# One kernel of attention, routed experts and a dense MLP: first group's rows gathered and prepared between conversions, two accumulations of the second product run beside the first group

## The chip, the cores and the metric

One Trainium2 chip, one core. The metric is the device time of one execution in microseconds (us), as the median of several runs. The engines: PE (TensorE: matmuls, and PEld its weight loads), DVE (VectorE), ACT (ScalarE), POOL (GpSimd), SP (SyncE, here a queue that issues DMAs).

## What is computed

```python
x = attention(q, k, v)                  # 4 batches, 12 heads, 448 rows, causal
# 8 experts, each row goes to the one with the largest gate logit
out[mask] = gate_w * eom * (relu(x[mask] @ w1[e]) @ w2[e])
# dense MLP on the 1792 rows of 768
h = out @ w_in                          # 768 -> 2048
g = h - tanh(h)
y = g @ w_out                           # 2048 -> 768
```

Weights come as 64-bit floats and are converted on the chip. A product of two matrices is done as three products of 16-bit planes (hi x hi, hi x lo, lo x hi), so every operand has a high and a low plane.

## The kernel before, in words

The kernel runs attention, then the experts one after the other in slots of 128 rows, then the dense MLP. The order of instructions on every engine is written by hand (`manual_schedule`): an engine takes its instructions in the order in which the program text issues them.

Beside the experts w_in and w_out are converted: 24 blocks of 128 x 1024 numbers, the first 12 of w_in, the rest of w_out. `conv` makes one block: three DVE operations put the 64-bit words together in the one buffer `cc` (`to_f32`, L896 to L902), `scaled` makes the high plane (L113 on ACT, L117 on DVE), `rest_of` the low plane (L115 and L129 on POOL, or L121 on DVE). `conv_store` writes both planes to the DRAM tensor `wb_d`; `wi_load` and `wo_load` bring quarters of w_in and w_out back. `remaining()` converts, in a loop whose length comes from the data, what the experts had no time for; here the loop is not entered. The last two blocks of w_out (q = 0, 1) are loaded from POOL's queue (1 MB each) and converted straight into w_out's buffer; q = 0 uses `cc` as well.

The last expert (e = 7) has its optional slots filled by `fill(z)`: fill(1) converts unit 0, fill(2) issues the two POOL loads and converts unit 1, fill(3) is `first_prep`. Rows of the first group of the MLP pass through prep0 (gather of sorted rows, SP, L971), prep1 (three reduces L982 and small operations, DVE), prep_hi (ACT, L996), prep_lo (POOL, two pairs L1010 and L1012 a block of rows), prep_sc, prep2 (transposes on PE, L149, and copies L151, L153) and prep3 (row scales through PE, L1036).

The MLP runs over five groups of 128-row blocks, GB = (3, 3, 3, 3, 2). Its loop has 16 steps n a group, one for each 128 of the 2048 columns. `a_mm(n)` (L1222) is 18 matmuls of 128 x 384 for h; `act_a` multiplies by the row scale into `cc` (L1230, called h below), squares and tanh go on ACT, V and X on POOL (L1232, L1235); `act_b`, `act_c` evaluate a polynomial on DVE (L1242, L1248, L1250) and write the high plane of g, `act_d` its low plane (L1258; POOL for group 0). The pool of h's PSUM has two buffers, so a_mm(n+2) waits for h of n. `mm2_step` (L1273) is three matmuls of 384 columns for y, one k of one accumulation; a group of three blocks has 2 x 3 x 16 = 96 of them, in six accumulations one after the other. They run one group behind the first product: while group 1's a_mm go, the 96 steps of group 0 are spread over its steps n = 17 to 31 (LAG = 1). So PE has no second product during group 0. While group 0 runs, group 1's rows are prepared (prep1 at n = 0, prep_hi and prep_lo at n = 1 to 7, prep2 at 9 to 11, prep3 at 12 and 13).

## Time and profile before

| | before |
|---|---|
| three runs, us | 1048.73, 1044.98, 1041.18 (median 1044.98) |
| the profiled execution, us | 1040.45 |
| its span, us | 1038.7 |
| PE busy | 984.5 us, 95% |
| DVE busy | 786.6 us, 76% |
| ACT busy | 596.7 us, 57% |
| POOL busy | 472.2 us, 45% |
| mean granted clock of PE | 0.993 |
| DMA, mean | 167 GB/s |

The span is the time between the first and the last instruction of the one execution that was profiled; the runs' times include what lies around it. Busy shares are averages over stages with different limits, so a stage has to be read by itself. Attention and experts fill the first 574 us, the MLP the rest.

### The profile page before, as it was taken

The numbers are of one execution on the slowest core, as the hardware profiler recorded it, in microseconds if no ns is written. First come the engines' busy times: TensorE is split into PE (matmuls) and PEld (weight loads), VectorE is DVE, ScalarE is ACT, GpSimd is POOL, SyncE is SP. The second block draws the span as 40 slices with busy tenths as digits, with TensorE's granted clock in tenths as the row PEclk, the third lists the DMA queues.
The fourth block names the chain that finished last, engine by engine and source line by source line (L and its number), as shares of the span: only waits on it lengthen the run. The fifth ranks groups of instructions, "written<-read, shape, count | busy, mean of one in ns | idle before, by whom it ended". The sixth has DMA issues, their size and how long they took to land. (4 is left out here: it accounts for less than half of the span.)

```text
span 1038.7 us, 24100 instructions
## 1 busy us (share of the span) xinstructions
PE 984.5 (95%) x9177; PEld 743.4 (72%) x9177; DVE 786.6 (76%) x1609; ACT 596.7 (57%) x1194; POOL 472.2 (45%) x499
## 2 busy tenths in 40 slices
PE   5999999998998999999988889999999999999996
PEld 4999999996876878777865555666666666667763
DVE  6668778786786778778877899887888798776640
ACT  5777776764456366564332679555656566555530
POOL 5475876585311011102137789545544443443321
PEclk9999999999999999999999999999999999999999
DMA  8989997963888979977987514010011000000000
GB/s 240 234 216 270 241 266 202 240 197 126 303 342 316 351 268 333 363 291 239 317 299 280 209 62 157 24 47 16 24 31 32 9 31 9 16 16 17 16 24 23
DMA packets 62646, 173.92 MB, mean 167 GB/s; under 512 B 8368, under 2 KB 23344, under 8 KB 59424
## 3 DMA queue, kind: packets, MB, share of 16 engines
q1 hardware_dynamic: 56352, 147.20, 42.7%
q0 software_dynamic: 6144, 24.84, 8.3%
q8 instruction: 79, 1.29, 0.5%
q14 instruction: 71, 0.58, 0.2%
HBM read 132.30 MB, written 29.62 MB: 156 GB/s over the span
## 5 line engine op out<-in xcount | busy, mean ns | idle before, releaser
L1273 PE MATMUL fo<-wo,g 128*128 128x384 f16 x1344 | 228.2, 326 | 0.0
L1222 PEld LDWEIGHTS <-raw 128*128 128x128 f16 x1440 | 140.7, 98 | 87.9 <-issue 9.5
L1273 PEld LDWEIGHTS <-g 128*128 128x128 f16 x1344 | 131.2, 98 | 83.8
L1232 POOL TENSOR_TENSOR V<-cu,cc 128x384 f32<-128x384 f32 (+1 forms) x80 | 78.7, 984 | 189.0 <-ACT cu L1231 188.2
L162 PEld LDWEIGHTS <-w 128*128 128x128 f16 x2592 | 148.9, 99 | 15.5 <-issue 14.4
L1222 PE MATMUL fh<-cu,raw 128*128 128x384 f16 (+1 forms) x864 | 131.9, 308 | 5.7 <-DVE cc L1230 5.7
L344 ACT ACTIVATE P<-s,nb 112x112 f32<-112x112 f32 (+1 forms) x192 | 89.9, 495 | 56.5 <-DVE nb L338 27.9
L381 PE MATMUL o<-v,PT 112*112 112x65 f32 x960 | 114.6, 259 | 0.0
L381 PEld LDWEIGHTS o<-v,PT 112*112 112x112 f32 x960 | 105.4, 178 | 0.1
L121 DVE SCALAR_TENSOR_TENSOR w<-raw,w 128x768 f16<-128x768 f32 (+1 forms) x99 | 99.1, 1061 | 3.6 <-ACT w L113 3.6
L799 POOL DMA_INDIRECT xg<-xs_d,idx x22 | 27.5, 1249 | 162.2 <-PEq L871 21.6
L1231 ACT ACTIVATE cu<-cc 128x384 f32<-128x384 f32 (+1 forms) x80 | 40.1, 502 | 101.9 <-DVE cc L1230 101.9
L1235 POOL TENSOR_TENSOR X<-cc,X 128x384 f32<-128x384 f32 (+1 forms) x80 | 91.2, 1141 | 4.1 <-ACT X L1234 0.5
L1230 DVE TENSOR_TENSOR cc<-fh,co 128x384 f32<-128x384 f32 (+1 forms) x80 | 42.0, 526 | 66.3 <-PE fh L1222 50.7
L113 ACT ACTIVATE w<-raw 128x768 f16<-128x768 f32 (+2 forms) x106 | 89.0, 904 | 5.5 <-DVE xi L758 3.2
L331 DVE TENSOR_REDUCE s<-s 112x2 f32<-112x224 f32 (+1 forms) x144 | 78.9, 548 | 14.8 <-PE s L327 12.7
L1242 DVE SCALAR_TENSOR_TENSOR V<-cu,V 128x384 f32<-128x384 f32 (+1 forms) x80 | 85.3, 1066 | 0.1
L1250 DVE TENSOR_TENSOR V<-V,co 128x384 f32<-128x384 f32 (+1 forms) x64 | 78.4, 1224 | 0.0
L1222 PE MATMUL fh<-yh,raw 128*128 128x384 f16 x384 | 67.6, 326 | 0.7 <-DVE cc L1230 0.7
L1251 ACT ACTIVATE g<-V 128x384 f16<-128x384 f32 (+1 forms) x80 | 40.1, 501 | 46.9 <-DVE V L1250 46.7
L362 PE MATMUL t<-ident,P 112*112 112x112 f32 x480 | 66.7, 262 | 0.0
L325 PE MATMUL s<-kh,qa 128*112 128x112 f16 (+1 forms) x192 | 54.7, 293 | 12.7 <-POOL qa L276 7.4
(657 smaller groups left out, 2038.8 us busy)
## 6 DMA issues: line engine op xcount, KB each, us to landing
raw<-w SPq DMA_DIRECT2D x48, 512.0 KB
raw<-w SPq DMA_DIRECT2D x60, 384.0 KB
cu<-wf SPq DMA_DIRECT2D x22, 1024.0 KB
wb_d<-co SPq DMA_DIRECT2D x22, 512.0 KB
raw<-kq SPq DMA_DIRECT2D x11, 896.0 KB
raw<-wb_d SPq DMA_DIRECT2D x8, 768.0 KB
xs_d<-xq SPq DMA_DIRECT2D x24, 224.0 KB
raw<-v SPq DMA_DIRECT2D x11, 448.0 KB
```

Source lines behind the costliest of these rows:

```text
L113: nc.scalar.activation(out=out, in_=in_, func=AF.Copy, scale=WS)
L121: nc.vector.scalar_tensor_tensor(out=out, in0=in_, scalar=WS, in1=hi, op0=ALU.mult, op1=ALU.subtract)
L162: nc.tensor.matmul(out=ph[:, (f % 4) * 128 : (f % 4 + 1) * 128], lhsT=w[0][:, ww, k, f * 128 : (f + 1) * 128], rhs=xTs[tag][:, xx, k, :], ...
L331: nc.vector.tensor_reduce(out=d["nm", m], in_=d["s", m], op=ALU.max, axis=AX.X, negate=True)
L344: nc.scalar.activation(out=d["P"][:, j, OFF[i] : OFF[i] + n], in_=d["s", m][:, z, :], func=AF.Exp, bias=d["nb"][:, 2 * i + j : 2 * i + j + ...
L381: nc.tensor.matmul(out=po[:, i, :], lhsT=d["PT"][:, g, o : o + CP], rhs=d["t"][3][:, hl, j, :], start=(j == 0), stop=(j == i))
L1222: nc.tensor.matmul(out=ph[:, 0:nt], lhsT=wi[ww][:, f // 4, k, f % 4 * 128 : (f % 4 + 1) * 128], rhs=yy[:, k, 0:nt], start=(q == 0), stop=( ...
L1232: nc.gpsimd.tensor_tensor(out=d["V"], in0=d["U"], in1=d["h"], op=ALU.mult)
L1235: nc.gpsimd.tensor_tensor(out=d["X"], in0=d["h"], in1=d["X"], op=ALU.subtract)
L1242: nc.vector.scalar_tensor_tensor(out=d["V"], in0=d[f"S{z}"], scalar=QD[z - 1], in1=d["V"], op0=ALU.add, op1=ALU.mult)
L1250: nc.vector.tensor_tensor(out=d["V"], in0=d["V"], in1=rs_y(g, nt), op=ALU.mult)
L1273: nc.tensor.matmul(out=po[:, 0:384], lhsT=t[:, x, k, i * 128 : (i + 1) * 128], rhs=wo_[ww][:, k, z * 384 : (z + 1) * 384], start=(k == 0 a ...
```

## The change

1. The three gathers of group 0 (prep0) are issued ahead of `remaining()`, whose scratch moves to another place (`spo`).
2. The fills of the last expert: fill(2) issues the two POOL loads and does `first_prep`; the conversion of unit 1 follows in fill(3).
3. Behind the last expert, the low planes of the last two blocks are made by DVE behind prep2 and prep3 instead of by POOL; `oidx` (the store addresses, two small POOL operations) is made in `order_b`.
4. The PSUM pool of the transposes has one buffer for each of two tags instead of two of one tag; `ro` takes one of them. prep2 of group 1 is done one plane a step at n = 7 to 12.
5. The order of the second product: the first 32 steps are two accumulations side by side (blocks 0 and 1, first half of the columns), two steps at each of n = 5 to 20. Their weights for k < 12 come from a copy of the first 384 columns of w_out in the buffer of g of group 1 (`wc_load`, four DMAs behind n = 0 and n = 1, 2.4 MB). The other 64 steps of group 0 are spread over n = 21 to 31. `wo_load` runs at n = 14 to 17, last quarter first, instead of n = 12 to 15.

```diff
     flg = cst.tile([1, 4], I32, name="flg")
+    oidx = cst.tile([128, NBLK, 2], U32, name="oidx")
...
-    def planes_T(rows, hi, lo, pool, tag="t", eng="a"):
-        for x, dst in enumerate((hi, lo)):
-            pt = pool.tile([128, 1024], F16, tag=tag, name=f"pt_{nc.get_next_instruction_name()}")
+    def planes_T(rows, hi, lo, pool, tag="t", eng="a", xs=(0, 1)):
+        for x in xs:
+            dst = (hi, lo)[x]
+            pt = pool.tile([128, 1024], F16, tag=tag[x % len(tag)], name=f"pt_{nc.get_next_instruction_name()}")
             pv = pt[:, 0:DM].rearrange("p (k n) -> p k n", k=KD)
...
-    def prep2(g, i, tag="t"):
+    def prep2(g, i, tag="t", xs=(0, 1)):
         d = G[g % 2]
         tsl = slice(i * 128, (i + 1) * 128)
-        planes_T(yq_of(g, i), d["yh"][:, :, tsl], d["yl"][:, :, tsl], tpool[0], tag, "v" if g == 1 else "a")
+        planes_T(yq_of(g, i), d["yh"][:, :, tsl], d["yl"][:, :, tsl], tpool[0], tag, "v" if g == 1 else "a",
+                 xs)
...
         nc.vector.tensor_reduce(out=smt[:, :, 1:2], in_=pv[:, :, 2:5], op=ALU.add, axis=AX.X)
+        for z in range(2):
+            nc.gpsimd.tensor_scalar(out=oidx[:, :, z], in0=smt[:, :, 0], scalar1=2.0, scalar2=float(z), op0=ALU.mult,
+                                    op1=ALU.add)
...
                 conv_load(stg[0], o)
-                conv(stg[0], stg[2][:, 0:1024], stg[2][:, 1024:2048])
+                conv(stg[0], spo[:, 0:1024], spo[:, 1024:2048])
                 nc.sync.dma_start(out=wb_d[:, :, ds(o, 1), :].rearrange("p a o n -> p a (o n)"),
-                                  in_=stg[2][:, 0:2048].rearrange("p (a n) -> p a n", a=2))
+                                  in_=spo.rearrange("p (a n) -> p a n", a=2))
...
             stg = [wof[0][:, z * 4096 : (z + 1) * 4096].bitcast(U32).rearrange("p (n t) -> p n t", t=2) for z in range(2)]
-            stg += [wof[1][:, z * 2048 : (z + 1) * 2048] for z in range(2)]
-            tot = nc.values_load(flg[0:1, 1:2], min_val=0, max_val=NDY)
-            remaining()
+            spo = wof[0][:, 8192:10240]
             first["yg"] = [wof[1][:, z * 2 * DM : (z + 1) * 2 * DM].bitcast(F32) for z in range(3)]
...
                 prep0(0, i, second * i if i else 0)
+            tot = nc.values_load(flg[0:1, 1:2], min_val=0, max_val=NDY)
+            remaining()
...
                         conv_load(stg[q], NDY + q, nc.gpsimd)
-                if z in (1, 2):
-                    conv(cu[z - 1], co[z - 1][:, 0], co[z - 1][:, 1], "p")
-                    conv_store(z - 1, nc.values_load(flg[0:1, z + 1 : z + 2], engines=(SP,), min_val=0, max_val=NDY - 1))
-                if z == 3:
                     first_prep()
+                if z in (1, 3):
+                    b = z // 2
+                    conv(cu[b], co[b][:, 0], co[b][:, 1], "p")
+                    conv_store(b, nc.values_load(flg[0:1, b + 2 : b + 3], engines=(SP,), min_val=0, max_val=NDY - 1))
...
         scaled("v", qhl[q][0], qc[q].bitcast(F32))
-        if q:
-            for prep in (prep2, prep3):
-                for i in range(GB[0]):
-                    tpool[0] = (mp_t, mp_y, mp_h)[i]
-                    prep(0, i, "tys"[i])
-        rest_of("p", qhl[q][1], qc[q].bitcast(F32), qhl[q][0])
+    for prep in (prep2, prep3):
+        for i in range(GB[0]):
+            tpool[0] = (mp_t, mp_y, mp_h)[i]
+            prep(0, i, "tys"[i])
+    for q in range(2):
+        rest_of("v", qhl[q][1], qc[q].bitcast(F32), qhl[q][0])
...
     fp_o = wctx.enter_context(tc.tile_pool(reuse_waits="tile", name="fp_o", bufs=2, space=PSUM))
-    tpool[0] = wctx.enter_context(tc.tile_pool(reuse_waits="tile", name="fp_t", bufs=2, space=PSUM))
-    oidx = yp.tile([128, NBLK, 2], U32, name="oidx")
-    for z in range(2):
-        nc.gpsimd.tensor_scalar(out=oidx[:, :, z], in0=smt[:, :, 0], scalar1=2.0, scalar2=float(z), op0=ALU.mult, op1=ALU.add)
+    tpool[0] = wctx.enter_context(tc.tile_pool(reuse_waits="tile", name="fp_t", bufs=1, space=PSUM))
     Q = {}
-    ro = fp_o.tile([128, 512], F32, tag="o", name="ro")
+    ro = tpool[0].tile([128, 512], F32, tag="r", name="ro")
     for i in range(GB[0]):
...
     steps = [(g, i, z, k) for g in range(len(GB)) for z in range(2) for i in range(GB[g]) for k in range(KF2)]
-    cur = [None]
+    KC = 12
+    AHEAD = {n: 2 for n in range(5, 21)}
+    steps[0:32] = [(0, i, 0, k) for k in range(KF2) for i in range(2)]
+    steps[32:96] = [(0, i, z, k) for i, z in ((2, 0), (0, 1), (1, 1), (2, 1)) for k in range(KF2)]
+    acc = {}
+    def wc_load(k0, k1):
+        for x in range(2):
+            src = wb_d[:, x, NI : NI + KC * DM // 1024, :].rearrange("p a n -> p (a n)").rearrange("p (k n) -> p k n", n=DM)
+            nc.sync.dma_start(out=gt[1][:, x, k0:k1, :], in_=src[:, k0:k1, 0:384])
     late = []
...
         if k == 0:
-            cur[0] = fp_o.tile([128, 512], F32, tag="o", name=f"fo_{bk}_{z}")
-        po = cur[0]
+            acc[bk, z] = fp_o.tile([128, 512], F32, tag="o", name=f"fo_{bk}_{z}")
+        po = acc[bk, z]
         t = gt[g % 2]
         for x, ww in ((0, 0), (0, 1), (1, 0)):
-            nc.tensor.matmul(out=po[:, 0:384], lhsT=t[:, x, k, i * 128 : (i + 1) * 128],
-                             rhs=wo_[ww][:, k, z * 384 : (z + 1) * 384], start=(k == 0 and x == 0 and ww == 0),
+            w = gt[1][:, ww, k, :] if bk < 2 and z == 0 and k < KC else wo_[ww][:, k, z * 384 : (z + 1) * 384]
+            nc.tensor.matmul(out=po[:, 0:384], lhsT=t[:, x, k, i * 128 : (i + 1) * 128], rhs=w, start=(k == 0 and x == 0 and ww == 0),
                              stop=(k == KF2 - 1 and x == 1))
...
             a_mm(n)
-            if n in (9, 10, 11):
-                prep2(1, (9, 10, 11).index(n))
+            if 7 <= n < 13:
+                prep2(1, (n - 7) // 2, xs=((n - 7) % 2,))
             for i in {12: (0, 1), 13: (2,)}.get(n, ()):
...
             wi_load(nc.sync, f + 1)
-        if g == 0 and f in (12, 13, 14, 15):
-            wo_load(nc.sync, f - 12)
+        if n in (0, 1):
+            wc_load(n * 4, 4 + n * 8)
+        if 14 <= n < 18:
+            wo_load(nc.sync, (3, 0, 1, 2)[n - 14])
         if 0 < g < len(GB) - 1:
...
                 if f == (5, 8, 12)[i]:
-                    prep2(g + 1, i)
+                    prep2(g + 1, i, "tr")
                 if f == (6, 9, 13)[i]:
                     prep3(g + 1, i)
-        if okf(n) and g >= 1 and f >= LAG:
-            tot = GB[g - 1] * 2 * KF2
-            q0 = tot * (f - LAG) // (KF2 - LAG)
-            q1 = tot * (f - LAG + 1) // (KF2 - LAG)
+        for _ in range(AHEAD.get(n, 0)):
+            mm2_step()
+        lag = 5 if g == 1 else LAG
+        if okf(n) and g >= 1 and f >= lag:
+            tot = GB[g - 1] * 2 * KF2 - (sum(AHEAD.values()) if g == 1 else 0)
+            q0 = tot * (f - lag) // (KF2 - lag)
+            q1 = tot * (f - lag + 1) // (KF2 - lag)
             for _ in range(q1 - q0):
...
```

On POOL, in the last expert's fills, before (co is the buffer of a converted unit, wo_17684 the buffer that holds the gathered rows and their planes):

```order
L906 DMA wo_17683<-wf 128x2048 x2
L115 TENSOR_SCALAR scm<-cc 128x512
L129 TENSOR_TENSOR co_4959<-scm,co_4959 128x512
L115 TENSOR_SCALAR scm<-cc 128x512
L129 TENSOR_TENSOR co_4959<-scm,co_4959 128x512
L1010 TENSOR_SCALAR scm<-wo_17684 128x384
L1012 TENSOR_TENSOR wo_17684<-scm,wo_17684 128x3x128
```

and now, up to the same conversion (lines are numbered two or one higher):

```order
L1012 TENSOR_SCALAR scm<-wo_17687 128x384
L1014 TENSOR_TENSOR wo_17687<-scm,wo_17687 128x3x128
L1012 TENSOR_SCALAR scm<-wo_17687 128x384
L1014 TENSOR_TENSOR wo_17687<-scm,wo_17687 128x3x128
L116 TENSOR_SCALAR scm<-cc 128x512
L130 TENSOR_TENSOR co_4960<-scm,co_4960 128x512
L116 TENSOR_SCALAR scm<-cc 128x512
L130 TENSOR_TENSOR co_4960<-scm,co_4960 128x512
```

The low half of unit 1's conversion stood ahead of all prep_lo pairs; now it is the last of them, and no low half of the last two blocks follows on POOL.

On SP, before, from the end of `remaining()` on (UNCONDITIONAL_BRANCH closes it; wo_17684 as above, ys_d the experts' rows):

```order
L1077 UNCONDITIONAL_BRANCH
L1126 TENSOR_LOAD flg
L1126 ISA x2
L971 DMA wo_17684<-ys_d 128x768
L971 ISA
L971 DMA wo_17684<-ys_d 128x768
L971 ISA
L971 DMA wo_17684<-ys_d 128x768
```

and now, up to the branch that opens it:

```order
L973 DMA wo_17687<-ys_d 128x768
L973 ISA
L973 DMA wo_17687<-ys_d 128x768
L973 ISA
L973 DMA wo_17687<-ys_d 128x768
L1133 TENSOR_LOAD flg
L1133 ISA x2
L1083 COMPARE_AND_BRANCH
```

The three gathers moved from behind the conditional loop to ahead of it.

On PE, in group 0, before, at the end of a_mm(5) (fh_5) and the start of a_mm(6) (each LDWEIGHTS loads the weights of the matmul behind it):

```order
L1222 LDWEIGHTS raw1_89
L1222 MATMUL fh_5_19711<-cu_1_4956,raw1_89 128x384
L1222 LDWEIGHTS raw1_89
L1222 MATMUL fh_5_19711<-cu_1_4956,raw1_89 128x384
L1222 LDWEIGHTS raw1_89
L1222 MATMUL fh_6_19747<-cu_0_4955,raw1_89 128x384
L1222 LDWEIGHTS raw1_89
L1222 MATMUL fh_6_19747<-cu_0_4955,raw1_89 128x384
```

and now, at the end of a_mm(5) (g_0 is g of group 0, g_1 the buffer with the copy of w_out; fo_0 and fo_1 are the two accumulations):

```order
L1225 LDWEIGHTS raw1_90
L1225 MATMUL fh_5_19709<-cu_1_4957,raw1_90 128x384
L1225 LDWEIGHTS raw1_90
L1225 MATMUL fh_5_19709<-cu_1_4957,raw1_90 128x384
L1287 LDWEIGHTS g_0_19483
L1287 MATMUL fo_0_0_19745<-g_1_19484,g_0_19483 128x384
L1287 LDWEIGHTS g_0_19483
L1287 MATMUL fo_0_0_19745<-g_1_19484,g_0_19483 128x384
L1287 LDWEIGHTS g_0_19483
L1287 MATMUL fo_0_0_19745<-g_1_19484,g_0_19483 128x384
L1287 LDWEIGHTS g_0_19483
L1287 MATMUL fo_1_0_19749<-g_1_19484,g_0_19483 128x384
```

Six matmuls of the second product stand between a_mm(5) and a_mm(6), and likewise behind each a_mm up to n = 20.

## Rows read from the trace of the kernel before

**Rows 1.** Windows: us; busy PE, PEld, DVE, ACT, POOL (instructions); granted clock, DMA share, GB/s

```profile
600.00:620.00 20.00, 17.55 (x126) 10.78 (x124) 20.00 (x33) 15.66 (x32) 17.48 (x16) 1.00 0.19 71
...
640.00:660.00 20.00, 20.00 (x125) 12.04 (x123) 18.82 (x36) 13.52 (x27) 13.12 (x12) 1.00 0.07 21
```

**Rows 2.** Waits of PE, 540 to 650 us: total us, times, longest

```profile
PE fh L1222 <- DVE cc L1230: 6.3, 8, 1.6
PE py_I-18271_18272 L174 <- ACT hh_I-18095_18096 L169: 4.1, 1, 4.1
```

**Rows 3.** Timeline of PE in group 0: start us, us, line, operation, [idle before]

```profile
591.35 3.08 PE L1222 MATMUL fh<-cu,raw 128*128 128x384 f16 x18 [1.65 <-DVE cc L1230]
...
609.21 0.50 PE L149 MATMUL pt_I-19869_19870<-identh,wo 128*128 128x128 f16 x6
...
621.93 0.27 PE L1036 MATMUL rsp_I-20025_20026<-wo,onesb 128*128 128x256 bf16 x1
...
632.89 2.11 PE L1222 MATMUL fh<-yh,raw 128*128 128x384 f16 x12 [0.35 <-DVE cc L1230]
```

**Rows 4.** Timeline of DVE, lead-in and start of group 0, columns as above

```profile
541.13 0.75 DVE L896 TENSOR_SCALAR cc<-cu 128x512 uint32<-128x512 uint32 x2
541.80 1.29 DVE L899 SCALAR_TENSOR_TENSOR cc<-cu,cc 128x512 uint32<-128x512 uint32 x2
...
555.48 0.95 DVE L982 TENSOR_REDUCE wo<-wo 128x1 f32<-128x768 f32 x1 [2.96 <-DMA wo<-ys_d]
...
562.83 0.69 DVE L896 TENSOR_SCALAR cc<-wo 128x1024 uint32<-128x1024 uint32 x1 [0.45 <-DVEq L871]
...
572.62 0.69 DVE L117 TENSOR_SCALAR wo<-wo 128x1024 f16<-128x1024 f32 x1
...
574.17 0.55 DVE L151 COPY cu<-pt_I-19457_19458 128x768 f16<-128x768 f16 x1
577.72 0.56 DVE L1230 TENSOR_TENSOR cc<-fh,co 128x384 f32<-128x384 f32 x1 [3.00 <-POOL scm L115]
...
590.75 0.54 DVE L1230 TENSOR_TENSOR cc<-fh,co 128x384 f32<-128x384 f32 x1
```

**Rows 5.** Timeline of POOL, the same stretch

```profile
559.61 0.59 POOL L1010 TENSOR_SCALAR scm<-wo 128x384 f32<-128x384 f32 x1
560.28 0.91 POOL L1012 TENSOR_TENSOR wo<-scm,wo 128x384 f16<-128x384 f32 x1
...
564.06 1.76 POOL L1012 TENSOR_TENSOR wo<-scm,wo 128x384 f16<-128x384 f32 x1
...
573.12 0.68 POOL L115 TENSOR_SCALAR scm<-cc 128x512 f32<-128x512 f32 x1 [1.61 <-DMA xg<-xs_d,idx]
...
579.73 1.16 POOL L129 TENSOR_TENSOR wo<-scm,wo 128x512 f16<-128x512 f32 x1
...
581.21 0.98 POOL L1232 TENSOR_TENSOR V<-cu,cc 128x384 f32<-128x384 f32 x1
...
594.16 1.63 POOL L1258 TENSOR_TENSOR g<-V,g 128x384 f16<-128x384 f32 x1
```

**Rows 6.** Timeline of SP, its DMA issues

```profile
546.61 1.56 SPq L971 DMA_DIRECT2D wo<-ys_d  x3
549.25 11.26 SPq L917 DMA_DIRECT2D wb_d<-co  x2
...
563.43 0.83 SPq L955 DMA_DIRECT2D raw<-wb_d  x2
```

**Rows 7.** Waits of SP's queue, 540 to 600 us

```profile
SPq L1077 <- SPq L1077: 4.0, 1, 4.0
```

**Rows 8.** Windows around PE's idle stretch ahead of the slot, columns as in group 1

```profile
558.00:560.00 2.00, 0.00 (x0) 0.00 (x0) 1.72 (x6) 2.00 (x3) 1.50 (x3) 1.00 0.18 68
...
562.00:563.00 1.00, 1.00 (x5) 0.48 (x4) 0.55 (x2) 0.00 (x0) 0.90 (x2) 0.50 1.05 395
```

**Rows 9.** Line L121 on DVE, 300 to 560 us: duration ns min/median/max

```profile
L121 DVE SCALAR_TENSOR_TENSOR co<-cc,co x32: 684/692/693, 311.5 to 530.7; 128x512 f16<-128x512 f32 x32
```

## The prediction

> **What bounds the kernel now.** I read the busy table by stretches first. From 640 us on PE is busy 20.00 of 20 us, and 125 matmuls of 384 columns fill the stretch: 0.16 us each [rows 1]. Nothing but less PE work, or PE idle time taken out ahead of it, can shorten the rest of the kernel. Between 600 and 620 us PE is busy 17.55 and DVE 20.00: there, in group 0, DVE is the bound [rows 1]. The waits of PE between 540 and 650 us then show what there is to win: 6.3 us in eight waits of fh for h (the DVE operation at L1230), and one wait of 4.1 us for hh, the relu of the last expert's second slot [rows 2]. PE's timeline places the first kind: blocks of 18 matmuls of 3.08 us, with gaps such as 1.65 us ahead of n=5 and still 0.35 us at n=16, which starts at 632.89 [rows 3]. Last I followed the lead-in on DVE, POOL and SP [rows 4 to 6].
>
> Group 0 starts with h0 at 577.72, after 3.00 us in which DVE waited for POOL's scm L115 [rows 4]: h is written to the buffer cc, which POOL still reads for the low half of the last converted w_out block. POOL's eight operations for that run from 573.12 to 580.9, and V of n=0 begins only at 581.21 [rows 5].
>
> **Gathers ahead of the conditional loop.** SP waits 4.0 us at the branch of `remaining()` [rows 7], ahead of the three gathers, the first of which goes out at 546.61 [rows 6]. Behind the change they leave about 4.5 us earlier, near 542. The third reduce now begins at 555.48, after a DMA wait of 2.96 us [rows 4], beside two 1 MB loads from POOL's queue; without these beside them I take the reduces as done by 549 and the scales by 550. (With the old 8.9 us from first issue to third reduce, 551.)
>
> **prep ahead of conversion 1.** ACT's prep_hi then ends near 552.5, DVE's conversion of unit 1 runs behind it, and hh comes near 557. The wait of 4.1 us [rows 2] goes, and with it the half clock: after PE stood empty at 558 to 560 us its granted clock was 0.50 at 562 to 563 us [rows 8]. Slot 7.2 thus ends some 5 us earlier. That is worth nothing by itself: what starts group 0 is the work behind it on DVE.
>
> POOL now runs six prep_lo pairs, then the low half of conversion 1. A pair takes 0.59 + 0.91 us plus gaps, 1.6 [rows 5]; conversion 1 takes 2 x (0.68 + 1.16) = 3.7 by the rows of the same operations [rows 5]. From 550 that is 550 + 9.6 + 3.7 = 563.3, with gaps 564. Beside DVE's long two-input operations the second half of a pair took 1.76 instead of 0.91 [rows 5]; if all six were stretched so, with the first halves in proportion, it is 6 x 2.9 + 3.7 = 21, hence 571. DVE's overlapping work is now mostly one conversion, not two blocks, so I take X = 566 for POOL's end, bounds 564 and 571.
>
> [...]
>
> **Conversions of the last two blocks.** DVE's to_f32 of q=0 overwrites cc, so it now waits for X. Uncontended, two blocks cost 2 x (0.75 + 1.29 + 1.29 + 0.69) = 8.0 us [rows 4]; before they took 562.83 to 573.3, 10.4 us [rows 4]. Then three copies of yl (0.55 each, 0.47 apart: 1.5 us [rows 4]) and the two rest_of moved from POOL: 0.69 us per 512 columns [rows 9], hence 1.3 each, 2.6 together. h0 comes at X + 12.1 = 578.1, against 577.72: **not earlier**, +0.4. Under the bounds of X it is 576.1 to 583.1.
>
> PE stands idle some 6 us ahead of a_mm(0), and the row above says that it then runs some us at half clock; the 12 matmuls that need only yh can start when w_in's first quarter has landed, so this is covered by the DVE work as long as that quarter comes by 574. SP issues it behind the store of conversion 1 (X + 0.3 = 566.3) and that store's landing. Before, the load at 563.43 followed 2.9 us after the issues of the stores ended (549.25 + 11.26 = 560.5) [rows 6]; so 569.5, and 1.57 MB at the 1 MB per 2.6 us of the neighbouring stretch (395 GB/s, [rows 8]) takes 4.0: 573.5 to 575. It is close, and costs at most 1.5 us.
>
> What POOL's freedom buys: V of n=0 follows its square at once instead of at 581.21, and the small DVE operations of group 1's prep1 no longer share with POOL. I put 1.0 us on that, so h of n=3 (590.75 [rows 4]) comes at 590.75 + 0.4 - 1.0 = 590.15.
>
> **The 32 ahead steps.** A step is three matmuls: 0.48 us. 22 of them stand at n=5 to 15, two per n, 10.6 us of work taken out of group 1, where PE is full [rows 1]. In group 0 PE then needs per n 18 + 6 matmuls, 2.9 + 0.97 = 3.87 us; eleven of them 42.6, with six batches of transposes of 0.50 and three rs matmuls of 0.27 (3.8 us, [rows 3]) 46.4. DVE's part per n is as before. So PE becomes the bound of group 0. From h3, a_mm(5) starts 0.6 later; to the 46.4 I add 1.5 for two stalls: the first ahead step needs the low plane of g(0), whose POOL operation stood at 594.16 and took 1.63 [rows 5], about as long as a_mm(5) now lasts; and the transposes have one PSUM buffer per tag instead of two. a_mm(16) starts at h3 + 48.5; before it was 632.89 - 590.75 = 42.1. So n=16 comes 6.4 later relative to h3 with 10.6 us of work done: gain 4.2.
>
> At n=16 to 20 ten more steps are taken. They only fill the gaps there (0.35 twice and the smaller, together 0.9 [rows 3]); I give 0.5 back for DVE being late at n=18 with group 2's preparation. The cost of the extra loads of w_out's half, 2.4 MB on SP's queue between the quarters of w_in: 6 us at the rate above. The second quarter goes first, the third is needed at n=8, the last at n=12, some 20 to 40 us later: hidden. Were it not hidden PE would wait up to 6 us at n=4.
>
> **Sum**: +0.4 (h0) - 1.0 (n=0 to 3) - 4.2 (n=5 to 15) - 0.9 + 0.5 = -5.2, rounded to -5. The profiled execution took 1040.45 us, 1.7 over its span; it lies 4.5 under the median of 1044.98 and 0.7 under the lowest. I forecast the median: 1044.98 - 5 = 1040.
>
> **Rivals.**
> (a) *Start later, nothing gained.* POOL's prep_lo and conversion 1 are stretched, X is 569 to 571, h0 3 to 5 us later. For it: 1.76 for 0.91 [rows 5]. Against: less DVE work beside it. Time 1043 to 1045.
> (b) *Slower.* The same chain, one mechanism: cc is now held by conversion 1 on POOL, DVE's last two blocks and the two rest_of lie serially behind it. It decides from an h0 over 5.2 us later, X beyond 571.2; that needs prep_lo to start after 550 too, as with the old landing. X = 573 gives 1047.
> (c) *The ahead steps gain nothing*: each step pair waits for a late low plane of g, because POOL, stretched by DVE, runs its act_d behind V and X (1.63 rather than 0.91). Group 0's PE idle stays, only elsewhere. Against: five n lie between g's start and its use. Only the start terms are left: 1044 to 1046.
> (d) *Start really earlier*: hh 5 us earlier carries through, with X at 564 or below and DVE's copies and rest_of partly in its own gaps. h0 at 573 to 576, 2 to 5 us ahead of my 578.1: -7 to -10; with neither of the two stalls of 1.5 us in all down to -12: 1033 to 1038.
>
> [...] Were a_mm(0) not covered by DVE's work, it would take 6.2 instead of 3.08 us, h0 would be 2 us later, and the gain 3 instead of 5.
>
> **How the numbers follow.** Forecast (-2 to -8): 0.54. (a) 0.15, (c) 0.09, (b) 0.09, (d) 0.13. One per cent, 10.4 us, is about what a measurement of this kernel can tell from no change: its three runs lie 7.5 us apart. Faster by over 1%: the better half of (d) and some luck in the median, 0.11. Slower by over 1%: only the tail of (b), X past 581, 0.04. Within: 0.85. The range reaches from 1032 (most of (d)) to 1046 (all of (a), part of (b) and (c)); the forecast's own is 1037 to 1043.
>
> **What would show it.** Right: hh without its 4.1 us wait; the first gather near 542; h0 within 2 us of 578; V of n=0 right behind its square; PE over 19 of 20 us between 600 and 640, and DVE under 20. Wrong: h0 past 583 (a, b) or before 576 (d); PE gaps that end on a POOL subtraction of g ahead of the ahead steps (c); a wait of fh for a load at n=0 or 4.

## The result and the profile after

The changed kernel is slower: 1055.26 us in the median of 17 runs against 1045.69 for the kernel before in its own 17, ratio 1.0078 with an interval of 1.0054 to 1.0102 (the ratio is not the quotient of the two medians, which is 1.0092). That is 8 to 10 us more, where 5 less were forecast, and outside the range of 1032 to 1046. All ratios here leave out executions in a slower state, among them two of ahead_short's twelve and one of start_early_nocc's at 1276 to 2627 us; the one trace of ahead_short is of such an execution, of 1056.99 us.

The profiled executions were 1055.61 (span 1053.9) and 1040.45 us (span 1038.7), 15.2 apart. The first lies at its median, the second 5 below its own, so some 5 of the 15.2 are scatter. Both traces have 9177 matmuls in the same stages. At the first matmul of the second product of the last expert's first slot (py of slot 7.1), called a below, the changed kernel is 2.9 us behind, in stages that the change hardly touches. The rest arises behind a.

The windows that answer [rows 1] (us; busy PE, PEld, DVE, ACT, POOL; granted clock, DMA share, GB/s), with the lead-in and group 1's start:

```profile
560.00:580.00 20.00, 12.06 (x80) 6.99 (x81) 14.12 (x17) 6.79 (x12) 14.00 (x15) 0.74 0.31 117
580.00:600.00 20.00, 15.55 (x90) 8.54 (x87) 13.37 (x23) 7.85 (x17) 4.30 (x4) 0.91 0.72 269
600.00:620.00 20.00, 17.26 (x110) 10.23 (x108) 20.00 (x38) 16.88 (x33) 16.35 (x14) 1.00 0.75 271
...
660.00:680.00 20.00, 15.48 (x103) 9.41 (x101) 18.07 (x34) 12.71 (x25) 11.89 (x11) 1.00 0.07 21
```

and of the kernel before:

```profile
560.00:580.00 20.00, 18.17 (x124) 10.79 (x125) 15.72 (x18) 7.57 (x16) 16.98 (x18) 0.91 0.65 231
...
660.00:680.00 20.00, 20.00 (x134) 12.32 (x132) 16.66 (x30) 11.17 (x22) 11.17 (x10) 1.00 0.06 21
```

Two things stand out: a lead-in in which PE is busy for 12.06 and 15.55 of 20 us, at a mean granted clock of 0.74 and 0.91, and a hole at 660 to 680 us, where PE was full before. The waits of PE from 535 us to the end (total us, times, longest) name both; the first and the third row answer [rows 2]:

```profile
PE py_I-18274_18275 L176 <- ACT hh_I-18098_18099 L171: 7.9, 1, 7.9
PE fo L1287 <- ACT ot L1291: 4.9, 1, 4.9
PE fh L1225 <- DVE cc L1233: 3.4, 3, 1.7
PE fh L1225 <- DMA raw<-wb_d: 2.3, 2, 1.4
...
PE fo L1287 <- POOL g L1261: 1.1, 1, 1.1
```

The wait for hh has not gone, it has doubled. The eight waits for h are three. New are two waits for the DMA of w_in's first quarter and one of 4.9 us for ot, the write-out of finished accumulations by ACT.

**The lead-in.** SP's timeline, in two pieces, then on (compare [rows 6]):

```profile
546.82 1.21 SPq L973 DMA_DIRECT2D wo<-ys_d  x2
...
553.10 0.35 SPq L973 DMA_DIRECT2D wo<-ys_d  x1
...
555.54 20.30 SPq L919 DMA_DIRECT2D wb_d<-co  x2
...
579.30 0.82 SPq L957 DMA_DIRECT2D raw<-wb_d  x2
```

The gathers go out ahead of the conditional loop, but the third leaves 5 us after the second. The store of conversion 1 ends its issue at 575.84, and w_in's first quarter is asked for at 579.30. POOL's timeline, against [rows 5]:

```profile
558.81 0.58 POOL L1012 TENSOR_SCALAR scm<-wo 128x384 f32<-128x384 f32 x1 [2.63 <-PE ph_I-18180_18181 L164]
...
573.59 1.67 POOL L130 TENSOR_TENSOR co<-scm,co 128x512 f16<-128x512 f32 x1
590.52 1.00 POOL L1235 TENSOR_TENSOR V<-cu,cc 128x384 f32<-128x384 f32 x1 [15.25 <-ACT cu L1234]
```

POOL starts its six pairs at 558.81, ends conversion 1 at 575.26 and then has nothing to do for 15 us. DVE's timeline, against [rows 4]:

```profile
556.67 0.95 DVE L984 TENSOR_REDUCE wo<-wo 128x1 f32<-128x768 f32 x1 [1.92 <-DMA wo<-ys_d]
...
573.54 0.70 DVE L898 TENSOR_SCALAR cc<-wo 128x1024 uint32<-128x1024 uint32 x1 [4.50 <-POOL scm L116]
...
584.63 1.22 DVE L122 SCALAR_TENSOR_TENSOR wo<-wo 128x1024 f16<-128x1024 f32 x1
589.26 0.56 DVE L1233 TENSOR_TENSOR cc<-fh,co 128x384 f32<-128x384 f32 x1 [3.42 <-PE fh L1225]
592.26 2.67 DVE L984 TENSOR_REDUCE wo<-wo 128x1 f32<-128x768 f32 x3 [2.44 <-SPq L873]
```

DVE waits 4.50 us until POOL has read cc (L116), is through with the last blocks at 585.85, and then waits another 3.42 us for a_mm(0). PE's timeline and its clock say why (compare [rows 3, 8]):

```profile
583.33 1.15 PE L1225 MATMUL fh<-cu,raw 128*128 128x384 f16 x6 [1.43 <-DMA raw<-wb_d]
585.36 9.65 PE L1225 MATMUL fh<-cu,raw 128*128 128x384 f16 x48 [0.88 <-DMA raw<-wb_d]
...
680.69 4.28 PE L1287 MATMUL fo<-wo,g 128*128 128x384 f16 x15 [4.91 <-ACT ot L1291]
```

```profile
586.00:588.00 2.00, 2.00 (x7) 0.88 (x6) 0.00 (x0) 0.00 (x0) 0.00 (x0) 0.50 0.76 297
```

a_mm(0) waits for the two planes of w_in, at 583.33 and 585.36, and then runs at a granted clock of 0.50 (586 to 588 us), after four microseconds, 582 to 586, in which PE was busy for 1.8.

**The hole behind a_mm(21).** DVE and ACT there (n = 19's h is the second DVE row; n = 20's chain on ACT begins at 676.34):

```profile
666.93 0.94 DVE L984 TENSOR_REDUCE co<-co 128x1 f32<-128x768 f32 x1
...
671.43 0.55 DVE L1233 TENSOR_TENSOR cc<-fh,co 128x384 f32<-128x384 f32 x1
```

```profile
676.34 0.52 ACT L1234 ACTIVATE cu<-cc 128x384 f32<-128x384 f32 x1 [0.41 <-DVE cc L1233]
...
680.08 1.03 ACT L1291 ACTIVATE ot<-fo,usc 128x384 f32<-128x384 f32 x2
```

a_mm(19) ends near 666.9, but DVE then does prep1, prep_lo and prep_sc of group 2 and comes to h(19) only at 671.43. ACT follows DVE, and its two ot stand in its order behind the chain of n = 20. Both accumulation buffers are held until ACT comes to them; PE, through with a_mm(21) and two batches of transposes, stands for 4.91 us and goes on at 680.69.

**Stages.** The table is worked out from the timelines of each kernel: a is the start of PE's first matmul of py of slot 7.1, h0, h3, ... are the starts of DVE's h operation (L1230; L1233 in the changed kernel), the end is the start of PE's last matmul (1029.70 before, 1044.86 after). us, one execution each; the ratio is that of the timed runs to those of the kernel before, with its 95% interval.

| kernel | ratio | a to h0 | h0 to h3 | h3 to h16 | h16 to h21 | h21 to h31 | h31 to end |
|---|---|---|---|---|---|---|---|
| before | 1 | 37.8 | 13.0 | 48.4 | 24.3 | 62.8 | 303.5 |
| before_again | | 35.7 | 13.7 | 48.4 | 24.2 | 62.8 | 303.5 |
| changed | 1.0078 (1.0054, 1.0102) | 46.5 | 14.3 | 51.7 | 24.3 | 62.3 | 303.0 |
| start_only | 1.0079 (1.0042, 1.0116) | 42.3 | 15.9 | 48.4 | 24.3 | 62.8 | 303.5 |
| fill_only | 1.0091 (1.0055, 1.0127) | 41.9 | 11.9 | 48.4 | 24.3 | 62.8 | 303.5 |
| gath_only | 0.9983 (0.9947, 1.0019) | 35.6 | 13.7 | 48.4 | 24.3 | 62.8 | 303.5 |
| rest_only | 0.9976 (0.9948, 1.0005) | 35.7 | 12.4 | 48.4 | 24.3 | 62.8 | 303.5 |
| start_early | 1.0033 (1.0000, 1.0066) | 39.3 | 14.2 | 48.4 | 24.2 | 62.8 | 303.5 |
| start_early_nocc | 1.0021 (0.9992, 1.0049) | 40.0 | 16.7 | 48.4 | 24.2 | 62.8 | 303.5 |
| start_conv_end | 1.0013 (0.9980, 1.0046) | 42.1 | 11.7 | 48.4 | 24.2 | 62.8 | 303.5 |
| ahead_only | 1.0046 (1.0014, 1.0078) | 36.2 | 13.3 | 51.7 | 24.3 | 62.3 | 303.0 |
| ahead_short | 1.0058 (1.0023, 1.0093) | 36.2 | 13.1 | 51.7 | 28.3 | 57.2 | 302.5 |
| ahead_late | 0.9938 (0.9903, 0.9974) | 36.2 | 13.1 | 51.7 | 19.8 | 62.3 | 303.0 |
| late_rest | 0.9956 (0.9924, 0.9989) | 36.5 | 11.7 | 51.7 | 19.8 | 62.3 | 303.0 |
| after_late | 1.0042 (1.0006, 1.0077) | 41.8 | 13.3 | 51.7 | 19.8 | 62.3 | 303.0 |
| after_early_late | 1.0020 (0.9995, 1.0045) | 40.1 | 13.8 | 51.7 | 19.8 | 62.3 | 303.0 |

From h3 on the stages of kernels with the same code there repeat to 0.1 us. Ahead of it they scatter: 2.1 us between two executions of the kernel before, 4.7 between the changed kernel and after_late, whose lead-in is the same code. Most of the 4.7 comes from ahead of the lead-in: SP issues its first gather at a + 4.1 in the changed kernel's trace and at a + 0.3 in that of after_late (a = 542.25), POOL starts its pairs at a + 16.1 and a + 12.5, and DVE's wait for a_mm(0) is 3.42 and 2.34 us. SP in after_late:

```profile
542.52 7.54 SPq L973 DMA_DIRECT2D wo<-ys_d  x3
```

### The profile page after: what moved, and what is told of

Read it like the earlier page. It is cut to its first block, busy times and chain, and to the rows that moved or that the text cites. A ratio compares the mean times of both kernels' runs of the same rounds, so it can differ in the third digit from the quotient of the medians.

```text
span 1053.9 us, 24088 instructions
## 1 busy us (share of the span) xinstructions
PE 988.9 (94%) x9177; PEld 746.1 (71%) x9177; DVE 781.3 (74%) x1611; ACT 596.4 (57%) x1194; POOL 461.4 (44%) x491
## 5 line engine op out<-in xcount | busy, mean ns | idle before, releaser
L1287 PE MATMUL fo<-wo,g 128*128 128x384 f16 x1272 | 218.2, 328 | 4.9 <-ACT ot L1291 4.9
L164 PEld LDWEIGHTS <-w 128*128 128x128 f16 x2592 | 150.3, 100 | 14.8 <-issue 13.7
L1234 ACT ACTIVATE cu<-cc 128x384 f32<-128x384 f32 (+1 forms) x80 | 40.1, 502 | 112.2 <-DVE cc L1233 112.2
L1233 DVE TENSOR_TENSOR cc<-fh,co 128x384 f32<-128x384 f32 (+1 forms) x80 | 42.1, 526 | 73.9 <-PE fh L1225 55.7
L333 DVE TENSOR_REDUCE s<-s 112x2 f32<-112x224 f32 (+1 forms) x144 | 78.8, 547 | 14.4 <-PE s L329 13.1
L1254 ACT ACTIVATE g<-V 128x384 f16<-128x384 f32 (+1 forms) x80 | 40.1, 501 | 43.1 <-DVE V L1253 42.8
```

The source lines that it names most:

```text
L164: nc.tensor.matmul(out=ph[:, (f % 4) * 128 : (f % 4 + 1) * 128], lhsT=w[0][:, ww, k, f * 128 : (f + 1) * 128], rhs=xTs[tag][:, xx, k, :], ...
L333: nc.vector.tensor_reduce(out=d["nm", m], in_=d["s", m], op=ALU.max, axis=AX.X, negate=True)
L1287: nc.tensor.matmul(out=po[:, 0:384], lhsT=t[:, x, k, i * 128 : (i + 1) * 128], rhs=w, start=(k == 0 and x == 0 and ww == 0), stop=(k == KF ...
```

## The experiments

Each starts from the kernel before, the changed one or another experiment. The diffs are cut to the lines that say what was changed; "..." stands for what is left out.

**start_only.** Before, with parts 1 to 3 of the change.

```diff
+            tot = nc.values_load(...); remaining()      # behind the three prep0
+                    first_prep()                        # fill(2)
+                if z in (1, 3): conv(...); conv_store(...)
+        rest_of("v", qhl[q][1], qc[q].bitcast(F32), qhl[q][0])
```

> Parts 1 to 3 alone (gathers ahead of the loop, prep ahead of conversion 1, low planes of the last two blocks on DVE), the second product as before. Theory S (the start is what costs): the 8 to 9 us by which a_mm(0) and h0 came later in the changed kernel are made here, so 5 to 9 us slower than before, 1051 to 1055; POOL's last conversion operation ends past 570, w_in's first quarter is loaded behind it, h0 comes 5 us or more later relative to the last expert's first slot. Theory A (the ahead steps cost, and the offset before group 0 is only scatter between executions): within 2 us of before, 1044 to 1048.

Measured 1050.84 us, ratio 1.0079: theory S. h0 comes 4.5 to 6.6 us later and h3 another 2 to 3. By the times the start alone costs as much as the whole change.

**ahead_only.** Before, with parts 4 and 5.

```diff
+    AHEAD = {n: 2 for n in range(5, 21)}
+        lag = 5 if g == 1 else LAG
```

> Parts 4 and 5 alone (two accumulations beside group 0, copy of half of w_out, PSUM split), the lead-in as before. Theory S: h of n=16 comes some 6 us later relative to n=3 with 10.6 us of work done, a gain of 4, and the wait of about 5 us for ot at n=21 with what lies around it gives 6 back: 0 to 3 us slower than before, 1045 to 1049, the wait there again. Theory A: 6 to 10 us slower, 1051 to 1056.

Measured 1049.09, ratio 1.0046: slower by more than S's upper end, less than A. The wait for ot is there again, 4.9 us. By stages it loses 3.3 (h3 to h16), nothing at h16 to h21, and gets 1.0 back: 2.3 us of net loss. Neither half of the change is faster by itself. Part 4 was not run without part 5.

**ahead_short.** As ahead_only, ahead steps only to n = 15.

```diff
-    AHEAD = {n: 2 for n in range(5, 21)}
+    AHEAD = {n: 2 for n in range(5, 16)}
-        lag = 5 if g == 1 else LAG
+        lag = LAG
```

> As ahead_only, but two ahead steps only at n=5 to 15 (22 steps), and the 74 others of group 0 spread over n=17 to 31, as the kernel before spread its 96. If the loss at n=18 to 21 is PE running out of work while DVE prepares group 2 (both accumulations held until ACT, behind DVE, writes them out), the wait for ot is gone and the gain of 4 to 5 us stays: 1040 to 1042. If the wait for ot comes from the pair of accumulations as such, it stays, some us long, wherever the pair ends: 1045 or more.

Measured ratio 1.0058 (1.0023 to 1.0093). Neither theory: the wait for ot is gone, but no gain came. From n = 17 the remaining steps go at five per n, catch up with g, and PE waits for the low plane from POOL (waits of PE, 640 to 720 us):

```profile
PE fo L1286 <- POOL g L1260: 2.6, 1, 2.6
```

The wait is another one in the same place (h16 to h21 takes 28.3 us). That PE runs out of work in one form or another while DVE is behind, pair or no pair, is what this suggests; ahead_late tests it.

**fill_only.** Before, with part 2 alone.

```diff
                 if z == 2:
+                    first_prep()
-                if z in (1, 2):
+                if z in (1, 3):
```

> Part 2 alone: first_prep in fill(2), conversion of unit 1 in fill(3). Theory S, the reordering itself costs: conversion 1 waits on POOL behind six prep_lo pairs, its store and the load of w_in's first quarter behind that, and q=0 on DVE behind cc: 4 to 8 us slower, 1049 to 1053. If the cost lies in the gathers or in DVE's two rest_of instead: within 2 us of before.

Measured 1053.16, ratio 1.0091: S. The exchange of first_prep and conversion 1 makes the late start by itself: a to h0 41.9 against 35.7 and 37.8. It gives back 1 to 2 us at h0 to h3.

**gath_only.** Before, with part 1 alone.

```diff
-            tot = nc.values_load(...); remaining()
             for i in range(GB[0]):
                 prep0(0, i, second * i if i else 0)
+            tot = nc.values_load(...); remaining()
```

> Part 1 alone: the three gathers ahead of the conditional loop. The 4 us wait of SP at the branch is then expected between the second and the third gather (three issues over 5.5 to 7.3 us instead of 1.6), so the third row block comes no earlier: between 1 us faster and 2 us slower than before. If the wait belongs to the branch and not to SP's instructions being fetched, the gathers take 1.6 us, 4 us earlier, and the kernel is 2 to 4 us faster.

Measured 1040.52, ratio 0.9983 (0.9947 to 1.0019): nothing to be told from 0, and the interval holds the times of both theories. The trace decides. Its three gathers, on SP:

```profile
546.17 6.98 SPq L971 DMA_DIRECT2D wo<-ys_d  x3
```

All eight kernels with part 1 spread the three over 5.4 to 7.5 us, those without it over 1.56 (ahead_late 2.68, with waits for DMAs). The wait of 4 us [rows 7] has moved from the branch to a place between two gathers, and the third reduce ends at a + 13.5, as in before_again.

**rest_only.** Before, with part 3 alone.

```diff
-        rest_of("p", qhl[q][1], qc[q].bitcast(F32), qhl[q][0])
+        rest_of("v", qhl[q][1], qc[q].bitcast(F32), qhl[q][0])
```

> Part 3 alone: the low planes of the last two blocks on DVE behind prep2 and prep3 instead of on POOL. h0 then waits for 2.6 us of DVE work instead of POOL's scm at 577.1, and V of n=0 no longer for POOL's 580.9: h0 about 0 to 1 us earlier, V 2 us earlier: 0 to 3 us faster than before, 1040 to 1043. If moving this work to DVE were the cost of the late start, it would be 3 us or more slower.

Measured 1041.31, ratio 0.9976 (0.9948 to 1.0005): the forecast's direction, just short of being told from 0. The trace has h0 where before_again has it (a + 35.7) and 1.3 us less from h0 to h3. Moving this work to DVE was not the cost.

**start_early.** start_only, with w_in's first quarter loaded in fill(2).

```diff
                     first_prep()
+                    wi_load(nc.sync, 0)
...
-            wi_load(nc.sync, 0)
```

> As start_only, with the load of w_in's first quarter issued in fill(2), ahead of the store of conversion 1. Theory L: in the changed kernel h0 waited for PE, which waited for this load behind the store (landing after DVE was already free) and then ran at half clock: h0 follows DVE's last rest_of within 1 us, and the kernel is 3 to 5 us faster than start_only. Theory C (the chain over cc, POOL, DVE alone decides): within 1.5 us of start_only.

Measured 1047.06, ratio 1.0033 (1.0000 to 1.0066), 0.46% below start_only. The two intervals overlap, so the times alone do not show the gain; the trace shows what theory L asked for. h0 now follows DVE's last rest_of without a wait (DVE's timeline):

```profile
585.14 1.22 DVE L122 SCALAR_TENSOR_TENSOR wo<-wo 128x1024 f16<-128x1024 f32 x1
586.39 0.56 DVE L1231 TENSOR_TENSOR cc<-fh,co 128x384 f32<-128x384 f32 x1
```

**start_early_nocc.** start_early, the first of the last blocks put together in a free quarter of w_in's buffer.

```diff
-    qc = (cc, wof[0][:, 8192:10240].bitcast(U32))
+    qc = (wif[0][:, 9216:11264].bitcast(U32), wof[0][:, 8192:10240].bitcast(U32))
```

> As start_early, and the first of the last two blocks is put together in a free quarter of w_in's buffer instead of cc, so DVE does not wait for POOL's conversion 1. If the chain over cc is the other half of the late start, h0 comes another 4 to 8 us earlier: 7 to 11 us faster than start_only, about 1040 to 1044, level with before or up to 2 us faster. If DVE is held by something else, or the late start is made further ahead (gathers, fetch), no more than 2 us faster than start_early.

Measured ratio 1.0021 (0.9992 to 1.0049): 1 us below start_early, not to be told from it, and not 4 to 8. DVE no longer waits for cc, but does the same work beside POOL's, in the first operation below at 1.81 instead of 1.23 us, and h0 is no earlier. (SP's first gather stands at a + 4.0 in this trace and at a + 0.4 in start_early's, POOL's pairs at a + 14.1 and a + 12.2, so up to 2 us of the missing gain may be scatter.) And the gathers for group 1, behind the store of conversion 1 on SP, are now what DVE waits for:

```profile
569.87 1.81 DVE L900 SCALAR_TENSOR_TENSOR raw<-wo,raw 128x1024 uint32<-128x1024 uint32 x1
...
589.50 2.67 DVE L983 TENSOR_REDUCE wo<-wo 128x1 f32<-128x768 f32 x3 [4.88 <-SPq L872]
```

**start_conv_end.** start_early_nocc, conversion 1 behind the last expert's slots.

```diff
-                if z in (1, 3):
-                    b = z // 2
+                if z == 1:
+                    b = 0
...
+    conv(cu[1], co[1][:, 0], co[1][:, 1], "p")
+    conv_store(1, ...)
     qc = (wif[0][:, 9216:11264].bitcast(U32), ...)
```

> As start_early_nocc, with conversion 1 and its store behind the last expert's slots instead of in fill(3), so that the relu hh and its low plane hl of slot 7.2 no longer stand behind it on ACT and DVE. If that is what is left of the late start, PE's wait for hh falls from 4 to 6 us to 2 or less and h0 comes 2 to 4 us earlier: 0 to 3 us faster than before. If the rest is the late third gather or the sum of work on DVE, no more than 1 us better than start_early_nocc, 1 to 3 us slower than before.

Measured ratio 1.0013 (0.9980 to 1.0046), neither one. PE's wait for hh fell to 1.1 us as the first theory wanted, but a_mm(0) then waits for DVE's copies of yl, behind three blocks of conversion:

```profile
575.85 14.39 PE L1225 MATMUL fh<-cu,raw 128*128 128x384 f16 x73 [5.83 <-DVE cu L152]
```

After that idle time PE's granted clock is 0.50 (574 to 580 us) and a_mm(0) takes 5.4 us instead of 3.08; DVE waits 2.45 us for it, and h0 is at a + 42.1. The wait for hh was thus not what held h0. That the sum of DVE's work behind the last slot holds it is what this points to; no run takes that work away.

**ahead_late.** ahead_only, with group 2's preparation two to four steps later.

```diff
-                if f == (0, 3, 7)[i]:
+                if f == ((0, 6, 9) if g == 1 else (0, 3, 7))[i]:
-                if f == (2, 6, 9)[i]:
+                if f == ((5, 8, 11) if g == 1 else (2, 6, 9))[i]:
-                if f == (5, 8, 12)[i]:
+                if f == ((7, 10, 13) if g == 1 else (5, 8, 12))[i]:
-                if f == (6, 9, 13)[i]:
+                if f == ((8, 11, 14) if g == 1 else (6, 9, 13))[i]:
```

> As ahead_only, with group 2's preparation two to four steps later (gathers at n = 16, 22, 25; prep1 and prep_lo at n = 21, 24, 27; prep2 at 23, 26, 29; prep3 at 24, 27, 30). If the 4.9 us wait for ot at n=21 is DVE's work on group 2 at n=18, which delays h(19), with it ACT and the write-out that frees both accumulation buffers, the wait falls below 1.5 us and the kernel is 3 to 6 us faster than ahead_only, 1043 to 1046 (1 slower to 2 faster than before). If the wait belongs to the pair of accumulations itself, it stays at 4 to 5 us and the time is that of ahead_only.

Measured 1040.57, ratio 0.9938 (0.9903 to 0.9974): faster than the kernel before, and 1.1% below ahead_only, more than the forecast. The wait for ot falls from 4.9 to 1.6 us (1.5 was the mark), h16 to h21 from 24.3 to 19.8. PE's waits from 640 us on:

```profile
PE fo L1286 <- ACT ot L1290: 1.6, 1, 1.6
```

The windows of 660 to 680 us, ahead_only first and this kernel in the second fence, show PE's hole closing:

```profile
660.00:680.00 20.00, 14.79 (x89) 8.62 (x88) 15.95 (x29) 12.27 (x25) 11.47 (x11) 0.91 0.12 39
```

```profile
660.00:680.00 20.00, 18.41 (x122) 11.26 (x121) 18.45 (x36) 13.62 (x27) 13.20 (x12) 1.00 0.12 39
```

The stages account for 4.5 of the 11 us between the two ratios; the rest is not explained by the traces, and the interval of the ratio is 0.35% wide to either side.

**late_rest.** ahead_late with part 3.

```diff
-        rest_of("p", qhl[q][1], qc[q].bitcast(F32), qhl[q][0])
+        rest_of("v", qhl[q][1], qc[q].bitcast(F32), qhl[q][0])
```

> ahead_late and part 3 together: ahead steps with group 2's preparation later, and the low planes of the last two blocks on DVE; the lead-in otherwise as before. If the gains add (about 6 and 2 to 3 us): 7 to 10 us faster than before, ratio 0.990 to 0.993. If both take out the same idle time: 4 to 6 us, no better than ahead_late.

Measured 1040.0, ratio 0.9956 (0.9924 to 0.9989), some 4 to 5 us faster than before. Its trace is the shortest from h0 on (h0 to h3 11.7), and 1.0 us shorter than ahead_late's from a to the end; the timed runs do not tell the two apart. From h0 to h3 part 3 gains 1.4 us here and 1.3 in rest_only (against before_again); whether the gains add stays open by the times.

**after_late.** The changed kernel, with the four edits of ahead_late, of which the second is

```diff
-                if f == (2, 6, 9)[i]:
+                if f == ((5, 8, 11) if g == 1 else (2, 6, 9))[i]:
```

> The changed kernel with group 2's preparation later, nothing else. If the two faults of the change are separate (late start; stall at n=21), the wait for ot of 4.9 us falls to some 1.6 us and only the start stays: about 0 to 4 us slower than before, ratio 1.000 to 1.004, against 1.0078 with the stall. If a late start alone explains the result, still 6 us slower or more.

Measured 1048.15, ratio 1.0042: the wait for ot falls to 1.6 us, the late start stays.

**after_early_late.** after_late with the line of start_early.

```diff
                     first_prep()
+                    wi_load(nc.sync, 0)
...
-            wi_load(nc.sync, 0)
```

> The changed kernel with both repairs: w_in's first quarter loaded ahead of the store of conversion 1, and group 2's preparation later. If the two faults are separate and the load accounts for half of the late start, as start_early against start_only says (0.46%), the ratio is 1.0042 - 0.0046, within 3 us of before on either side. If the load's gain is lost beside the ahead steps, it stays at 1.004.

Measured 1044.64, ratio 1.0020 (0.9995 to 1.0045), within 3 us of before. Both repairs together bring the changed kernel level with the one before, not below it: h0 is still at a + 40.1, where before_again has it at a + 35.7.

**before_again.** The kernel before, unchanged.

> The kernel before, unchanged, for a second trace: how far the same stages lie apart between two executions. From the last expert's first slot to the end of the kernel they should agree within 1 us; the stages ahead of it may differ by several.

Measured 1044.79. From h3 on it agrees to 0.1 us; at a it is 5.9 us later, and a to h0 takes 2.1 us less, more than the 1 us expected. The trace on which the prediction rested had a late slot 7.1 to 7.2: PE's wait for hh, 4.1 us there, is 1.9 here.

## Why the prediction was wrong, step by step

**The step that failed first: a_mm(0) "covered by the DVE work".** My sum for h0 was X + 12.1, with DVE as the last to be ready, and w_in's first quarter "close", at most 1.5 us. In us behind a:

| kernel | POOL's pairs start | X | DVE through | DVE's wait for a_mm(0) | h0 |
|---|---|---|---|---|---|
| predicted | 10.1 | 26.1 | 38.2 | 0 to 1.5 | 38.2 |
| fill_only | 10.7 | 27.2 | 37.9 | 4.03 | 41.9 |
| start_only | 12.4 | 28.8 | 39.4 | 2.94 | 42.3 |
| after_late | 12.5 | 28.9 | 39.5 | 2.34 | 41.8 |
| start_early | 12.2 | 28.7 | 39.3 | none | 39.3 |
| changed | 16.1 | 32.5 | 43.1 | 3.42 | 46.5 |

In fill_only the scales come as early as I had them and X lies in my range (a + 24.1 to a + 31.1), and h0 is still late, by DVE's wait (rest_of stays on POOL there, and DVE's blocks and copies beside it, without the two rest_of, take 10.7 us from X, where the changed kernel takes 10.6 with them):

```profile
585.56 0.56 DVE L1230 TENSOR_TENSOR cc<-fh,co 128x384 f32<-128x384 f32 x1 [4.03 <-PE fh L1222]
```

In the changed kernel the wait is for landing and half clock together: the last 12 matmuls of a_mm(0) take 3.8 us, at a granted clock of 0.50 from 586 to 589 us, where 12 take 2.11 [rows 3]. I had the first 12 hang on the load alone. In start_only and the changed kernel PE does wait for the load (2.1 and 2.3 us). In fill_only, where h0 stands 4.9 us behind the start of a_mm(0) at 580.65, the profile puts PE's wait down to DVE's first copy of yl (L151), in after_late 1.54 us to that copy and 0.70 to the load:

```profile
PE fh L1222 <- DVE cu L151: 3.8, 1, 3.8
```

start_early, with the load early, has DVE's wait gone. Of my signs of being wrong two came, h0 past 583 and a wait of fh for a load at n = 0.

**The trace I subtracted from.** h0 stood at a + 37.8 in it; before_again, gath_only and rest_only have it at a + 35.6 to 35.7. My + 0.4 was thus + 2.5 against the kernel's other executions, before any term failed.

**Gathers.** "They leave about 4.5 us earlier" took the wait at the branch for the branch's own. The traces point to SP's instructions being fetched: in the gap of the kernel before, and again in the gap of the changed one between its second and third gather, one packet of the queue that brings instructions lands (DMA queues in 548.8 to 553.1 us of the changed kernel: queue, kind, packets, MB, share):

```profile
q14 instruction: 1, 0.01, 0.4%
```

No wait on a semaphore fills the 4 us of either gap, and gath_only shows that the wait stays when the branch is moved behind the gathers; that the packet is SP's, and that its fetch is the cause, is my inference and not shown. In the changed kernel the third gather was issued at a + 10.4 instead of my a + 3.6, and POOL's pairs, which need the scales, started at 558.81, a + 16.1, not a + 10.1. Of these 6 us, 3.6 are that trace's own (a + 12.5 in after_late).

**hh and the half clock.** Predicted gone, the wait became 7.9 us, and PE's granted clock was 0.50 behind it (566 to 570 us). Behind late scales stood prep_hi, conversion 1 on DVE (three pairs of operations from 560.83 to 566.04, 5.2 us beside POOL's pairs, where unit 0's took 3.2, from 543.99 to 547.14) and its high planes on ACT, and only then hh. I had put hh at 557 because I had the gathers early; the order that I described made it dependent on them. For h0 it mattered little: fill_only, with the early scales, waits 2.6 us for hh and has h0 where start_only has it.

**X.** I took 566; it was 575.26 in the changed kernel, 572.4 without the offset at a, above my 571, but a + 27.2 to 28.9, within the range, in fill_only, start_only and after_late. Pairs and conversion took 12.0 and 4.3 us in the changed kernel, together within half a microsecond of the 16 that I had allowed from 550 to 566. DVE did not wait for X itself but for POOL's last read of cc, 1.7 us ahead of it, and needed 12.3 us from there for my 12.1: it was through at X + 10.6, so the sum was 1.5 us too long here, which hid part of the late X. Rival (b) had the place and the sign, POOL's conversion holding what follows, and I had given it 0.09; that SP's queue hangs on it as well as DVE's, through the store, was in the text but not in its price.

start_early_nocc says more: without the shared cc only about 1 us was won by the times, not to be told from 0: beside each other the operations of both engines took longer (on DVE 1.81 us, where 1.23 stands at 576.38 in the changed kernel with POOL idle; on POOL 2.00 for L130, where it takes 1.16 at 549.04 in the same trace), and the gathers of group 1 hang on the same store.

**h0 to h3.** The 1.0 us from POOL's freedom is real where SP is not late: part 3 takes 13.7 (before_again) to 12.4 (rest_only) and 13.1 (ahead_late) to 11.7 (late_rest). In the changed kernel it was lost to prep1's wait of 2.44 us for group 1's gathers.

**The ahead steps, n = 5 to 15.** Right to a tenth: a_mm(16) started at 652.06, h3 at 603.53, 48.5 apart as predicted, and none of the three waits for h that are left lies between a_mm(5) and a_mm(16). The tenth is luck: the stalls were 1.1 us for the low plane of g(0) and 1.1 ahead of the row-scale matmuls at n = 12, where I had 1.5 for g and the transposes.

**n = 16 to 21.** Here the sum broke. I booked the 10.6 us taken out of group 1 as won, "where PE is full". It was full because its steps were there, 6.4 for each n. Without them PE's work at n = 17 to 20 falls to 3.9 us for each n, less than what DVE needs with group 2's preparation, and the idle time that had left n = 5 to 15 came back there. h16 to h21 takes 24.3 us before and after, though PE has some 7 us less to do; that the two are equal is chance. I gave 0.5 for DVE being late there; it is 4.5, by what ahead_late gets back from moving that preparation alone (19.8). In all: + 3.3, + 0.0, - 0.5, - 0.5 from h3 to the end, a loss of 2.3 where the sum had a gain of 4.6. Even ahead_late's stages gain 2.2 of the 4.6: its PE still waits 1.6 us for ot and 0.9 ahead of a row-scale matmul, where the kernel before waits 0.7 from a_mm(16) to the end.

**Transfers.** The copy of half of w_out cost nothing, as said: no wait of PE for a load lies behind n = 0.

**Chances.** Slower by over 1% had 0.04 and rival (b), "Slower", 0.09; the ratio is 0.8% up. Two terms that I took as small had one cause each that could be read from the order: what a_mm(0) waits for behind the late conversion, and DVE's load at n = 18.

The runs do not settle everything: the timed ratios and the single traces differ by 5 to 7 us for one kernel (fill_only: 0.9% by the times, 2.9 to 4.5 us from a to the end). The two halves cost 0.79% and 0.46% by themselves and 0.78% together. And with both repairs h0 is still 2 to 4 us later than in the kernel before.

## What to carry to other kernels

Work taken out of a stage in which an engine is full is a gain only down to the next engine's load in that stage; price the stage again with the work gone, and move the other engine's work before claiming the rest. When two tasks on one engine are exchanged, follow the one that is now last through every queue that waits for it, its store and the loads behind that store too. A wait of an instruction queue that no semaphore explains may belong to the position in the program: here moving the gathers ahead of it moved the wait between them and brought the last no earlier (gath_only: the three issues spread over 6.98 us, the third reduce done at a + 13.5, as in before_again). And read a second trace of the kernel before: here the stage from a to h0 was 2 us longer in the one than in the other.

## What the runs showed of the hardware

SP stood still for 4.0 us at a branch (kernel before, 541.6 to 545.6) and for 4.2 us in the middle of straight code (changed kernel, 548.8 to 553.0), while a single packet of the instruction queue q14 landed in each stretch; in before_again and fill_only the wait at the branch was 3.5 and 3.4 us. PE's granted clock fell to 0.50 in the changed kernel's lead-in twice, within PE's idle 7.9 us ahead of py (0.92 at 560 to 562 us, 0.50 from 562) and in a_mm(0), after 582 to 586 us, in which PE was busy for 1.8 us (0.50 at 586 to 588); the last 12 of that a_mm's 18 matmuls, 3.08 us for all 18 otherwise, then took from 585.36 until near 589. DVE's operations of 128x1024 with two inputs took 1.49 to 2.07 us beside POOL (1.49 and 1.82 at 563.55 and 565.08 in the kernel before, 2.07 at 574.27 in the changed one, with POOL at work until 575.26) and 1.23 alone (576.38 in the changed kernel).
